# Engine orders from a list scheduler, q and k as six tokens a partition, decay as a bias of the exponentials: one change to a fused attention and channel-mix kernel

## The chip, the cores and the metric

One core of a Trainium2 chip. The metric is the device time of one execution in microseconds (us), median of several runs. A ratio leaves slow runs out: it is the mean time of one kernel's fast runs over the mean time of the kernel before's fast runs in the same rounds on the same chip, so it is not quite the ratio of the medians quoted beside it. The versions ran on several chips and in several rounds, so where two of them are close, the ratios compare them better than the medians.

## The reference, cut to what matters

```python
# q, k, v: 8 batches x 8 heads x 576 tokens x 64, float32;  f: 8 x 8 x 576
scores = scale * q @ k.T
cum    = cumsum(log(clip(f, 1e-4, 1)))
scores = where(causal, -1e9, scores + cum[i] - cum[j])     # decay
attn   = softmax(scores) @ v                               # -> x: 8 x 576 x 512
# channel mix, with x_prev = x one token earlier
xk = mu_k * x + (1 - mu_k) * x_prev;   xr likewise with mu_r
out = sigmoid(xr @ w_r) * (relu(xk @ w_k) ** 2 @ w_v)      # w_k 512x1024, w_v 1024x512, w_r 512x512
```

q and k are drawn with a standard deviation of 0.1, so the scores are tiny beside the decay.

## The kernel before

Two heads (a "pair") are worked together, 32 pairs in all, and the channel mix of a batch ("keys", "gates", "value blocks") runs between the attention of later batches. Loads arrive in float32 with one token of 64 numbers (256 bytes) as a row; other engines cast them. Decay comes in as a weight: v is multiplied by exp(-cum) on GpSimd, and the columns of E that give the row sums hold the same weights.

```python
def load(src, t, Pi, eng=None):                    # 64-number rows, float32, from SyncE's queue
    ...
        (eng or nc.sync).dma_start(out=t[:, :, hh, :],
            in_=src[b, h0 + hh, :4 * P, :].rearrange("(c p) d -> p c d", p=P))

def transposes(Pi):                                # ten 128x128 transposes, one eviction
    ...
    nc.vector.tensor_copy(qkT[Pi % NQK], tp[:, :, 0:640])          # written contiguously

def scores(Pi, ti):
    ...                                            # exponentials of both heads in one instruction
    nc.scalar.activation(out=a[:, :, off:off + w], in_=sc[:, :, 0:w], func=AF.Exp, scale=SCALE)

def vw_pair(Pi):                                   # decay into v
    nc.gpsimd.tensor_tensor(out=vw[Pi % NV], in0=vf[Pi % NV], in1=wbf[...], op=ALU.mult)

for s in range(NP + LAG):                          # the order of all engines, slot by slot
    ...
    scores(s, 0); mask(s, 0); scores(s, 1); ...
    run_gv(value_unit)
    transposes(s + 1)
    run_keys(2 * more)
    ...
```

The reciprocals of the row sums go out to DRAM once a batch and come back spread over the partitions (`scr`, then `rb`).

The softmax here doesn't subtract the row's maximum and nothing guards it: scores larger than these inputs give would overflow.

## Time and profile before

| | before |
|---|---|
| median of the first three runs | 356.54 us (354.05 to 358.79) |
| span of the profiled run | 356.4 us |
| first unit of the channel mix ("key") starts | 77.0 us |

The page, the windows, the timeline and the waits that carry the reading are quoted in the prediction. Three more groups of the page matter for what follows; the columns are line, engine, operation, output and input, shapes, count, then busy us, mean ns of one, then the idle time just before them and what ended it.

```profile
L255 ACT ACTIVATE a<-sc 128x1024 bf16<-128x1024 f32 (+2 forms) x128 | 102.2, 836 | 39.1 <-PE sc L249 39.0
L173 POOL TENSOR_TENSOR vw<-vf,wbf 128x512 bf16<-128x512 f32 x32 | 35.4, 1107 | 18.4 <-DMA vf<-in_v_dram 12.4
L192 DVE COPY qkT<-tp 128x1280 bf16<-128x1280 bf16 x32 | 26.1, 815 | 21.3 <-PE tp L191 21.3
```

The reader should note the last: one eviction of transposed q and k, 1,280 bf16 elements a partition, costs VectorE 815 ns, and there are 32.

### The profile page before, as it was taken

What the parts mean: (1) busy time and instruction counts of PE and PEld (TensorE: products, weight loads), DVE (VectorE), ACT (ScalarE), POOL (GpSimd) and SP (SyncE); (2) the same over time, 40 slices, a digit from 0 to 9 for tenths busy, and PEclk for the clock granted to TensorE, in tenths of its full rate; (3) what the DMA queues carried; (4) which work ended last, traced back from release to release, by engine and by line L of the source; (5) the groups of instructions that cost most, each with busy time, mean ns of one, the idle gap of its engine ahead of it and who ended that gap; (6) DMA issues with size and microseconds to landing.
All of it is one profiled execution on the core that took longest, in us unless ns stands there. A gap on an engine that the chain in (4) does not pass through costs nothing.

```text
span 356.4 us, 7440 instructions
## 1 busy us (share of the span) xinstructions
PE 285.3 (80%) x2853; PEld 172.9 (49%) x2853; DVE 220.2 (62%) x438; ACT 175.8 (49%) x296; POOL 158.2 (44%) x256
## 2 busy tenths in 40 slices
PE   1377573575998899888997899789978974898995
PEld 1255342354665456535664556456645542555562
DVE  5511307772889577844885889558857764558442
ACT  1567352346476556515774666356746621233451
POOL 2177375574547464725464656435653520100000
PEclk9999995669899999969999999999999989699999
DMA  9799979929963995499429971997284306420112
GB/s 162 142 180 207 200 181 209 193 56 215 197 148 89 219 234 135 104 235 187 121 81 189 235 189 62 206 228 190 62 183 114 97 17 151 93 89 31 61 59 88
DMA packets 132355, 52.02 MB, mean 146 GB/s; under 512 B 116384, under 2 KB 127136, under 8 KB 132320
## 3 DMA queue, kind: packets, MB, share of 16 engines
q1 hardware_dynamic: 128560, 48.39, 63.4%
q0 software_dynamic: 2096, 2.62, 4.5%
q10 hardware_dynamic: 1664, 0.54, 0.8%
q8 instruction: 22, 0.36, 0.5%
q14 instruction: 13, 0.11, 0.1%
HBM read 43.14 MB, written 11.01 MB: 152 GB/s over the span
## 4 chain that ended last, share of the span: by engine, by line
PE 55%; DVE 21%; DMA 11%; ACT 5%; issue 3%; SPq 3%; POOL 1%; DVEq 0%; POOLq 0%; ACTq 0%
PE kp L357 15%; PE vp L369 12%; PE rp L369 6%; PE num L322 6%; PE sc L249 5%; DMA rb<-scr 5%; PE den L282 4%; DVE xr L346 4%; PE tp L191 3%; DVE qkT L192 3%; ACT rel L361 3%; DMA kf<-in_k_dram 3%; DVE relusq L362 2%; ACT a L255 2%; PE vp L373 2%
## 5 line engine op out<-in xcount | busy, mean ns | idle before, releaser
L267 POOL TENSOR_SCALAR_AFFINE_SELECT a<-a 128x256 bf16<-128x256 bf16 (+2 forms) x128 | 68.5, 549 | 120.6 <-ACT a L255 101.0
L255 ACT ACTIVATE a<-sc 128x1024 bf16<-128x1024 f32 (+2 forms) x128 | 102.2, 836 | 39.1 <-PE sc L249 39.0
L361 ACT ACTIVATE rel<-kp 128x288 bf16<-128x288 f32 x128 | 52.6, 411 | 90.0 <-PE kp L357 84.0
L357 PE MATMUL kp<-xk,wk_sb 128*128 128x288 bf16 x512 | 79.8, 300 | 9.8 <-ACT rel L361 4.5
L249 PE MATMUL sc<-qkT 64*128 64x192 bf16 (+4 forms) x512 | 44.3, 280 | 26.0 <-DVE qkT L192 18.0
L328 DVE TENSOR_TENSOR x<-num,rb 128x384 bf16<-128x384 f32 x64 | 27.2, 458 | 59.9 <-DMA rb<-scr 38.3
L362 DVE TENSOR_TENSOR relusq<-rel 128x288 bf16<-128x288 bf16 x128 | 52.5, 430 | 18.1 <-ACT rel L361 17.7
L357 PEld LDWEIGHTS <-wk_sb 128*128 128x128 bf16 x512 | 48.9, 101 | 29.5 <-issue 14.2
L369 PE MATMUL vp<-wv_sb,relusq 128*128 128x512 bf16 x256 | 61.5, 384 | 0.0
L249 PEld LDWEIGHTS <-qkT 64*128 64x128 bf16 x512 | 23.4, 102 | 53.0 <-issue 45.3
L173 POOL TENSOR_TENSOR vw<-vf,wbf 128x512 bf16<-128x512 f32 x32 | 35.4, 1107 | 18.4 <-DMA vf<-in_v_dram 12.4
L383 ACT ACTIVATE th<-rp 128x512 f32<-128x512 f32 x36 | 21.5, 597 | 37.7 <-PE rp L369 33.8
L390 DVE SCALAR_TENSOR_TENSOR res<-th,vp 128x512 f32<-128x512 f32 x36 | 24.5, 680 | 24.1 <-PE vp L369 13.4
L192 DVE COPY qkT<-tp 128x1280 bf16<-128x1280 bf16 x32 | 26.1, 815 | 21.3 <-PE tp L191 21.3
L369 PEld LDWEIGHTS <-relusq 128*128 128x128 bf16 x256 | 23.8, 99 | 29.3 <-issue 1.6
L322 PE MATMUL num<-a,vw 128*64 128x192 bf16 (+3 forms) x448 | 31.2, 284 | 6.2 <-DVE x L328 6.2
L369 PE MATMUL rp<-wr_sb,xr 128*128 128x512 bf16 x128 | 33.7, 387 | 2.5 <-ACT rel L361 2.5
L346 DVE SCALAR_TENSOR_TENSOR xr<-diff,mu_r_sb,x 128x576 bf16<-128x576 bf16 x32 | 31.2, 976 | 0.0
L346 DVE SCALAR_TENSOR_TENSOR xk<-diff,mu_k_sb,x 128x576 bf16<-128x576 bf16 x32 | 28.4, 887 | 1.1
L191 PE MATMUL tp<-ident,qb 128*128 128x128 bf16 x128 | 14.2, 242 | 16.5 <-ACT a L255 6.7
L322 PEld LDWEIGHTS <-vw 128*64 128x64 bf16 x448 | 21.1, 119 | 13.0 <-issue 7.9
L163 POOL CAST qb<-qf 128x512 bf16<-128x512 f32 x30 | 18.7, 624 | 7.9 <-DMA qf<-in_q_dram 7.9
(55 smaller groups left out, 219.5 us busy)
## 6 DMA issues: line engine op xcount, KB each, us to landing
out_dram<-res SPq DMA_DIRECT2D x36, 256.0 KB, 2.9
qf<-in_q_dram SPq DMA_DIRECT2D x64, 128.0 KB, 4.0
vf<-in_v_dram SPq DMA_DIRECT2D x64, 128.0 KB, 3.6
kf<-in_k_dram SPq DMA_DIRECT2D x62, 128.0 KB, 4.0
rb<-scr SPq DMA_DIRECT2D x16, 384.0 KB, 5.1
rb<-scr SPq DMA_DIRECT2D x16, 192.0 KB, 5.9
scr<-R SPq DMA_DIRECT2D x8, 192.0 KB, 1.9
tail_f<-in_q_dram SPq DMA_DIRECT2D x8, 128.0 KB, 4.8
```

Source lines behind the costliest of these rows:

```text
L173: nc.gpsimd.tensor_tensor(out=vw[Pi % NV], in0=vf[Pi % NV], in1=wbf[:, :4, 2 * Pi:2 * Pi + 2].unsqueeze(3).to_broadcast([P, 4, 2, D]), op= ...
L192: nc.vector.tensor_copy(qkT[Pi % NQK], tp[:, :, 0:640])
L249: nc.tensor.matmul(sc[:, hh, col - off:col - off + n], lhsT=t[lo:lo + D, 1, kb * P:(kb + 1) * P], rhs=t[lo:lo + D, 0, q0:q0 + n], start=Tr ...
L255: nc.scalar.activation(out=a[:, :, off:off + w], in_=sc[:, :, 0:w], func=AF.Exp, scale=SCALE)
L267: nc.gpsimd.affine_select(out=v_, in_=v_, compare_op=ALU.is_ge, fill=0.0, base=0, pattern=pat, channel_multiplier=-1)
L322: nc.tensor.matmul(nm[hh * D:(hh + 1) * D, q0 - o:q0 - o + w], lhsT=t[:, kb, hh, :] if kb < 4 else tl[:, 2 * p + hh, :], rhs=a[:, hh, col: ...
L328: nc.vector.tensor_tensor(out=xs[Pi % NX][:, 1 + o:1 + o + n], in0=nm[:, 0:n], in1=rbs[Pi][:, o:o + n], op=ALU.mult)
L346: nc.vector.scalar_tensor_tensor(out=dst[:, p, :], in0=diff, scalar=mu[:, p:p + 1], in1=x[:, 0:S], op0=ALU.mult, op1=ALU.add)
L357: nc.tensor.matmul(kp[:, :HB], lhsT=wk_sb[:, db, fb * P:(fb + 1) * P], rhs=xks[b][:, db, hf * HB:(hf + 1) * HB], start=(db == 0), stop=(db ...
L361: nc.scalar.activation(rel, kp[:, :HB], func=AF.Relu)
L362: nc.vector.tensor_mul(rsq[b][:, fb, hf * HB:(hf + 1) * HB], rel, rel)
L369: nc.tensor.matmul(ps, lhsT=tiles[b][:, i, t0:t0 + P], rhs=w[:, i, :], start=(i == 0), stop=(i == n - 1))
```

## The change

Its intent: TensorE is idle for long stretches because the engines' orders are fixed slot by slot; so let a small program plan all orders from durations, dependences and buffers. Along with it come changes meant to lighten the other engines. Loads cast on the way (issued by GpSimd), q and k come six tokens to a partition, so that a row is 1,536 bytes in DRAM instead of 256, and decay becomes the bias operand of the exponential, so that v needs no scaling. The diff, cut to its core (cuts marked with three dots):

```diff
-    for s in range(NP + LAG):          # order written by hand, slot by slot
-        ...
+class Plan:                            # takes the ready step of the earliest rank ("tt") on each engine
+    def run(self, switch, bias): ...   # from durations, dependences and free buffers
+SIZES = dict(sc=2, mm=3, den=1, a=7, qkT=3, rb=2, v=5, vt=3, qk=8, rel=3, th=3, res=4, x=3, diff=2)
+SET = dict(lead=8, first=5526, fast=57, pace=6478, ... vlead=1129, qlead=4583, ...)   # ranks
+def graph(g, X=None):
+    ...
+    x = load("load_qk", (n, t), "POOL", 950, 1000 * len(pairs), ...)      # issue ns, transfer ns
+    x = load("load_v", (n,), "POOL", 1000, 1400 * len(pairs), when(i) - g["vlead"], ...)
+    EV[i].append(op("evac", (i, t), "DVE" if v else "ACT", 640 if v else 540, 130, ...))
+    ...
-        (eng or nc.sync).dma_start(out=t[:, :, hh, :], in_=...)           # float32
+        self.nc.gpsimd.dma_start(out=self.buf("qk", ("qk", n, t))[:, :w].rearrange("p h j d -> p h (j d)"),
+                                 in_=self.qk_in[t][b, h0:h0 + w].rearrange("h (p j) d -> p h (j d)", p=PT))
-            nc.tensor.transpose(tp[:, i, c * P:(c + 1) * P], in_, ident)   # 10 a pair
-    nc.vector.tensor_copy(qkT[Pi % NQK], tp[:, :, 0:640])
+                self.nc.tensor.transpose(o[hh * D:(hh + 1) * D, j * PT:(j + 1) * PT], src[:, h + hh, j, :],
+                                         self.ident, tile_position=(0, hh * D))   # 24 a pair
+    def evac(self, i, t):              # puts the tokens back in order: p*6+j <- j*96+p
+        o = self.buf("qkT", ("qkT", i))[:, t * S:(t + 1) * S].rearrange("c (p j) -> c j p", j=JT)
+        s_ = self.buf("mm", ("t", i, t)).bitcast(BF16)[:, :S].rearrange("c (j p) -> c j p", j=JT)
+        if t == 1 or i < EARLY:
+            self.nc.vector.tensor_copy(o, s_)
+        else:
+            self.nc.scalar.activation(out=o, in_=s_, func=AF.Copy)
-    nc.scalar.activation(out=a[...], in_=sc[...], func=AF.Exp, scale=SCALE)       # 4 a pair
+        self.nc.scalar.activation(out=..., in_=..., func=AF.Exp,                  # 10 a pair
+                                  bias=self.bias[:, kb, 2 * i + hh:2 * i + hh + 1], scale=1.0 / D ** 0.5)
-    nc.gpsimd.tensor_tensor(out=vw[Pi % NV], in0=vf[Pi % NV], in1=wbf[...], op=ALU.mult)
```

Batch 0 also gets its reciprocals spread by a float32 selection matmul (`pick`) instead of the trip through DRAM. The transposes leave token p·6+j at column j·96+p. The copy loops over j outside and p inside, on both sides: it reads the PSUM tile straight through and writes 2-byte elements at a step of six elements, 12 bytes.

## The prediction

> **What bounds the kernel now.** I read the page first (span, busy shares, the 40 slices, the chain), then the windows, then the timeline of one steady stretch, then the waits.
>
> ```profile
> span 356.4 us, 7440 instructions
> ...
> PE 285.3 (80%) x2853; PEld 172.9 (49%) x2853; DVE 220.2 (62%) x438; ACT 175.8 (49%) x296; POOL 158.2 (44%) x256
> ...
> PE   1377573575998899888997899789978974898995
> ...
> PEclk9999995669899999969999999999999989699999
> ...
> PE 55%; DVE 21%; DMA 11%; ACT 5%; issue 3%; SPq 3%; POOL 1%; DVEq 0%; POOLq 0%; ACTq 0%
> ```
>
> TensorE carries 55% of the chain, so no engine bounds all of it: 45% is hand-over. The slices show three stages: until about 90 us TensorE is half busy and partly at a lowered clock; then dense but not full; at the end dense with holes. The windows put numbers to it (columns: stretch, length, busy us of PE, PEld, DVE, ACT, POOL; clock; DMA share; GB/s):
>
> ```profile
> 0.00:91.00 91.00, 51.79 (x579) 34.39 (x581) 41.53 (x88) 41.79 (x54) 48.78 (x92) 0.86 0.94 175
> 91.00:290.00 199.00, 178.30 (x1902) 107.11 (x1902) 145.53 (x275) 113.23 (x197) 107.34 (x163) 0.97 0.72 156
> 290.00:356.40 66.40, 55.24 (x380) 31.39 (x380) 33.18 (x76) 20.73 (x45) 2.10 (x2) 0.94 0.25 77
> ```
>
> Busy time flatters TensorE because its records overlap. What work occupies it is better read from start to start, in the timeline and the chain in order of time (start, length, what):
>
> ```profile
> 232.37 0.61 PE L249 MATMUL sc<-qkT 64*128 64x384 bf16 x10
> ...
> 241.62 0.61 PE L249 MATMUL sc<-qkT 64*128 64x384 bf16 x10
> ...
> 245.95 0.53 PE L282 MATMUL den<-a,E 128*4 128x384 bf16 x16
> ...
> 246.41 0.85 PE L322 MATMUL num<-a,vw 128*64 128x384 bf16 x14
> ...
> 247.22 1.03 PE L357 MATMUL kp<-xk,wk_sb 128*128 128x288 bf16 x7
> ```
> ```profile
> 97.22 0.98 PE kp L357 x8
> ...
> 313.92 0.86 PE rp L369 x4
> 314.78 1.73 PE vp L369 x8
> ```
>
> Row sums take 0.46 us a pair (245.95 to 246.41), values 0.81; two key units 0.98, so 0.49 each; a gate 0.86, a value block 1.73. One pair with its share of the mix occupies a slot of 9.25 us (232.37 to 241.62). Its work: transposes 0.56, scores 0.43 and about 0.25, sums 0.46, values 0.81, four keys 1.96, 1.125 gates 0.97, 1.125 value blocks 1.95: 7.4 us. So a steady slot fills TensorE to 80%.
>
> Waits and durations used below:
>
> ```profile
> DVE x L328 <- DMA rb<-scr: 38.3, 14, 8.9
> ```
> ```profile
> 20.36 0.94 POOL L230 DMA_DIRECT2D wk_sb<-in_moe_w_k_dram  x1
> ...
> 24.65 0.77 POOL L230 DMA_DIRECT2D wr_sb<-in_moe_w_r_dram  x1
> ...
> 30.70 0.90 POOL L230 DMA_DIRECT2D wv_sb<-in_moe_w_v_dram  x1
> ```
>
> VectorE stands 38 us in 14 waits for the reciprocals that travel through DRAM, and a casting DMA costs GpSimd about 0.87 us to issue (mean of three).
>
> **What the Trainium skill says.** "Perfetto Trace Analysis", Identifying the Most-Contended Engine, says that matmul busy time is a poor measure of distance to the roofline; the trace agrees, 90% busy in the middle window against the 80% worked out above. "TensorEngine Tiling (Array Packing)", Key Properties, says that changing the tiling mode drains TensorE. The trace fits: values are 1,600 columns for each of two heads side by side, 0.67 us at the 0.86/2048 us per column of a gate, and take 0.81, so about 0.1 us goes at the change. "DMA: Bandwidth & Descriptors", SWDGE vs HWDGE vs iDMA, says that a casting DMA must be issued from GpSimd, where cores write its descriptors; hence the 0.87 us. "ScalarE: Activation LUTs", What ACT_TABLE_LOAD costs, says that a pointer operand adds about 93 ns to an ACTIVATE. The trace agrees: two of 64x576 take 682 ns without a bias tile (L203) and 774 with one (L207), 92 more. Whether this shows in back-to-back throughput no row tells.
>
> **The change part by part.**
>
> TensorE. Removed: ten 128-wide transposes a pair. Added: 24 of 96 columns on two column halves, six of them end to end per tensor: by the gate's rate 0.24 us, with many short starts I take 0.31, so 0.62 a pair against 0.56. Scores use the same 1,600 columns a head (0.7 us), but the first four pairs do the heads apart (four times 0.43 more). Sums and values have the same columns. The boundary block at row 512 of two batches becomes an ordinary one. Batch 0 gets eight fp32 selections, about 4 us together, in place of a trip through DRAM. Sum without drains: keys 128 x 0.49 = 62.7; gates 36 x 0.86 = 31; value blocks 36 x 1.73 = 62.3; attention 32 x (0.62 + 0.70 + 0.40 + 0.70) = 77.4; early heads 1.7; selections and bias 4.5: 240 us. Mode changes: I count about six a pair (transposes, values, scores twice, sums, back to full size), 32 x 6 x 0.1 = 19 us. TensorE needs about 259 us. So the arithmetic is not what shrinks; the idle time is.
>
> Start. Before, the mix starts at 91 us. Now decay needs no scaled v and no weighted sum columns, exponentials start as soon as the bias is there, the scheduler sends eight pairs ahead, and batch 0 normalises after two pairs and without DRAM. My estimate for the first key unit: bias at about 10 us, four pairs of exponentials at 3.4 to 4.3 us each until about 26, norm, selection and four pairs of mixing on VectorE (about 2.9 us a pair by its rows) until 33 to 38. In this time TensorE has about 18 us of attention work, so some 16 us are lost, where the first 91 us of before lost some 60.
>
> Middle and end. Reciprocals are asked for long before they are needed, so the 38 us of waits should go. The two engine orders are merged by a scheduler that knows a duration for each step; static buffers (seven exponential tiles, eight q/k tiles, rings of 3) let attention run ahead. At the end only the last block's chain remains: evict, store with 2.9 us to landing: 4 us. The 12 us hole at 294 to 305, one trip through DRAM, is covered by queued mix.
>
> GpSimd. Removed: casts 18.9 + 18.7 + 8.3, scaled v 35.4 + 8.3, in all 90 us. Added: 34 q/k loads, 64 v loads, 8 tails, 5 weights at 0.87 us: 97 us. Masks become 160: 128 at 0.50 and 32 at 0.42, 77 us for 68.5. About 178 us: no relief, though below 259. Loads of q and k go from 73,728 rows of 256 B to 12,288 of 1,536 B.
>
> ScalarE. The forms 128x1024, 128x768, 128x384 last 1023, 806, 493 ns: 0.83 ns a column and 175; two back to back take 1.94 us, so an instruction occupies 0.83 a column and about 72. Ten a pair of 3,200 columns in all: 3.37 us, 108 in total. The bias tile may add 92 ns each, 29 us. With 128 relus at 0.31, 36 tanh at 0.5, 28 evictions at 0.55 and the spreads: 183 to 212 us.
>
> VectorE. Squares go from 128 (52.5 us) to 64 of 128x576 at about 0.52 (33 us); scaling wv and the casts go, four more evictions come: about 200 us.
>
> Sum: 259 of TensorE + 16 at the start + 4 at the end = 279 with perfect packing. Against that, six mode changes a pair may be too many (some fall into idle time, some steps lie side by side): minus 8. For imperfect packing in the middle I add 2%, 5 us. Predicted: 276 us.
>
> **The rivals.**
>
> A, the ScalarE bound: if the bias operand costs throughput, a pair with its share of relu, tanh and eviction takes about 6.6 us while attention runs; TensorE needs about 7.9. So it would be a near second and disturb the order: 280 to 290 us. For it: 92 ns more in L207. Against: there was no neighbour to overlap with.
>
> B, GpSimd's queue: masks stand in order behind load issues. If an issue costs well over 0.87 us (a v load has 512 short pieces), or is held at a buffer, masks come late, sums and values wait, and the static order stalls: 290 to 310 us. For it: the scheduler's table gives one v group of four loads 1.0 us where these rows say 3.5. Against: 1,024 pieces of weights cost no more than 512.
>
> C, short transposes do not overlap: 24 weight loads a pair at about 56 ns rather than 26 add 0.7 us a pair, 23 us: near 298 us.
>
> D, packing is better than I grant: if drains mostly vanish and the first keys start by 28 us, 255 to 262 us.
>
> **Range and chances.** D and a mild A or C span 258 to 296 us. To reach the old time minus 2%, 349 us, idle time would have to stay at 90 us of 349, which needs two rivals at full size. Faster 0.95, same 0.03, slower 0.02.
>
> **What would show it.** Keys starting near 35 us; TensorE's share of the chain above 75%; the wait of VectorE for the reciprocals near zero; a steady pair with its mix in about 8 us; clock near full after 30 us. A is right if exponentials follow each other at over 0.6 us for 576 columns; B if GpSimd's issue rows exceed 100 us and TensorE waits for masks; C if transposes of one tensor take over 0.5 us. I am wrong altogether if start-to-start times of keys and value blocks grow, or if the start still takes over 60 us.

## The result, and the profile after

| | before | after |
|---|---|---|
| median (4 runs each, same chip) | 355.83 us (354.05 to 358.79) | 372.75 us (371.63 to 373.39) |
| ratio, 95% interval | | 1.045 (1.0386 to 1.0514): slower |

The prediction, 276 us, was wrong by 97 us and in its sign. Head of the page of the changed kernel, its slices of TensorE, and its chain by engine:

```profile
span 369.9 us, 8111 instructions
...
PE 293.9 (79%) x3141; PEld 167.9 (45%) x3141; DVE 235.9 (64%) x376; ACT 260.3 (70%) x525; POOL 151.2 (41%) x281
...
PE   2463597589859888689589986888878899999995
...
PEclk9999998879987999999989996999989999999998
...
PE 51%; ACT 25%; DVE 13%; issue 5%; POOL 4%; DMA 1%; ACTq 0%; DVEq 0%; POOLq 0%
```

TensorE's share of the chain fell from 55% to 51%, and ScalarE, 5% before, now holds 25% of it. The slices show a start of some 75 us at about half density, as before, then mostly eights and nines. ScalarE's busy time went up by 84.5 us (175.8 to 260.3). Two of the groups below raised it, the exponentials (102.2 us before) and ScalarE's share of the evictions; the one between them holds VectorE's evictions:

```profile
L490 ACT ACTIVATE a<-sc,bias 128x576 bf16<-128x576 f32 (+2 forms) x320 | 155.1, 545 | 52.1 <-PE sc L468 50.3
...
L461 DVE COPY qkT<-mm 128x576 bf16<-128x576 bf16 x36 | 73.5, 2082 | 30.0 <-PE mm L454 24.9
...
L463 ACT ACTIVATE qkT<-mm 128x576 bf16<-128x576 bf16 x28 | 58.5, 2089 | 5.5 <-PE mm L454 4.8
```

An eviction of 576 elements takes 2.08 us on either engine, where 1,280 elements took 0.815 us before. All 64 cost 132 us of two engines instead of 26 us of one. What that does to the order is in the chain in order of time (start, length, what), of the changed kernel in its middle:

```profile
81.06 2.09 ACT qkT L463
...
88.60 1.26 ACT a L490 x2
89.87 1.98 ACT qkT L463
91.84 1.00 ACT a L490 x2
...
97.03 1.26 ACT a L490 x2
98.30 1.97 ACT qkT L463
```

Once a pair the path runs through ScalarE: two exponentials, the eviction, two exponentials. Nothing behind the eviction in ScalarE's order starts for 2 us. And until it ends, the eviction holds the PSUM buffer that it reads, one of three (`mm`) that transposes, keys, gates and value blocks share. The timeline of a later stretch shows a key unit waiting for just such a buffer (in brackets: idle before, and what ended it):

```profile
192.80 2.09 ACT L463 ACTIVATE qkT<-mm 128x576 bf16<-128x576 bf16 x1
...
194.95 1.63 PE L591 MATMUL mm<-xk,wk 128*128 128x288 bf16 x12 [1.38 <-ACT qkT L463]
```

To see the whole span in one sum I split it by the start times of the trace's matmuls. A matmul that lasts over 1.15 times the usual of its form counts as run at half clock, and half of its time is the loss; a gap is from the modelled end of one matmul to the start of the next. The usual is the form's median. This is an estimate, good to a few us. In us:

| | before | after | loops exchanged (e1) | order searched (e14) |
|---|---|---|---|---|
| before the first matmul | 5.6 | 5.4 | 5.4 | 5.2 |
| TensorE's work at full clock | 256.1 | 267.3 | 267.8 | 270.1 |
| lost to half clock | 28.8 | 26.1 | 24.8 | 19.1 |
| gaps up to 80 us | 30.0 | 29.1 | 27.7 | 15.3 |
| gaps after 80 us | 31.7 | 37.4 | 14.7 | 7.1 |
| after the last matmul | 3.8 | 4.1 | 4.1 | 4.1 |
| span of the profiled run | 356.4 | 369.9 | 344.9 | 321.0 |

The first column of differences, before to after, says where the 13.5 us came from: 11 us more work on TensorE and 6 us more gaps after 80 us, against 3 us less loss to the clock. And it says where the expected gain did not appear: the gaps at the start stayed at 29 us, and those of the middle, which the scheduler was to close, grew.

### The profile page after: what moved, and what is told of

Read it like the earlier page. It is cut to its first block, busy times and chain, and to the rows that moved or that the text cites.

```text
span 369.9 us, 8111 instructions
## 1 busy us (share of the span) xinstructions
PE 293.9 (79%) x3141; PEld 167.9 (45%) x3141; DVE 235.9 (64%) x376; ACT 260.3 (70%) x525; POOL 151.2 (41%) x281
## 4 chain that ended last, share of the span: by engine, by line
PE 51%; ACT 25%; DVE 13%; issue 5%; POOL 4%; DMA 1%; ACTq 0%; DVEq 0%; POOLq 0%
PE mm L616 15%; PE mm L591 14%; ACT a L490 11%; ACT qkT L463 11%; PE sc L468 7%; PE mm L606 6%; DVE qkT L461 6%; PE mm L556 4%; PE mm L454 3%; POOL a L497 2%; ACT rel L595 2%; PE den L512 2%; DVE x L564 1%; PE mm L527 1%; POOL v L404 1%
## 5 line engine op out<-in xcount | busy, mean ns | idle before, releaser
L490 ACT ACTIVATE a<-sc,bias 128x576 bf16<-128x576 f32 (+2 forms) x320 | 155.1, 545 | 52.1 <-PE sc L468 50.3
L497 POOL TENSOR_SCALAR_AFFINE_SELECT a<-a 128x256 bf16<-128x256 bf16 (+1 forms) x160 | 70.1, 454 | 128.4 <-ACT a L490 122.9
L461 DVE COPY qkT<-mm 128x576 bf16<-128x576 bf16 x36 | 73.5, 2082 | 30.0 <-PE mm L454 24.9
L591 PE MATMUL mm<-xk,wk 128*128 128x288 bf16 x512 | 76.3, 293 | 11.8 <-ACT qkT L463 11.3
L616 PE MATMUL mm<-wv,sq 128*128 128x512 bf16 x288 | 74.6, 403 | 2.9 <-ACT qkT L463 2.6
L595 ACT ACTIVATE rel<-mm 128x288 bf16<-128x288 f32 x128 | 52.4, 429 | 27.3 <-PE mm L591 23.8
L468 PE MATMUL sc<-qkT 64*128 64x64 bf16 (+4 forms) x384 | 47.9, 301 | 25.3 <-ACT a L490 13.7
L591 PEld LDWEIGHTS <-wk 128*128 128x128 bf16 x512 | 49.2, 100 | 35.0 <-issue 16.7
L463 ACT ACTIVATE qkT<-mm 128x576 bf16<-128x576 bf16 x28 | 58.5, 2089 | 5.5 <-PE mm L454 4.8
L404 POOL DMA_DIRECT2D v<-in_v_dram x64 | 47.8, 765 | 9.5 <-PE mm L556 3.9
L626 DVE SCALAR_TENSOR_TENSOR res<-th,mm 128x512 f32<-128x512 f32 x36 | 25.3, 703 | 29.1 <-PE mm L616 24.3
L564 DVE TENSOR_TENSOR x<-mm,rb 128x384 bf16<-128x384 f32 (+1 forms) x64 | 27.7, 466 | 16.1 <-PE mm L556 12.8
L512 PE MATMUL den<-a,ones 128*4 128x192 bf16 (+4 forms) x512 | 19.4, 263 | 11.3 <-POOL a L497 11.3
```

Of the source, the lines that this page charges most:

```text
L404: self.nc.gpsimd.dma_start(out=t[:, :, h, :], in_=self.v_in[b, h0 + h, :4 * P, :].rearrange("(c p) d -> p c d", p=P))
L461: self.nc.vector.tensor_copy(o, s_)
L463: self.nc.scalar.activation(out=o, in_=s_, func=AF.Copy)
L468: self.nc.tensor.matmul(o, lhsT=t[lo:lo + D, S + kb * P:S + (kb + 1) * P], rhs=t[lo:lo + D, q0:q0 + n], start=True, stop=True)
L490: self.nc.scalar.activation(out=self.buf("a", ("a", i))[:, hh, KOFF[kb]:KOFF[kb] + n], in_=self.buf("sc", ("s", i, tok))[:, o:o + n], func ...
L497: self.nc.gpsimd.affine_select(out=v_, in_=v_, compare_op=ALU.is_ge, fill=0.0, base=0, pattern=[[0, 2], [1, n]], channel_multiplier=-1)
```

## The experiments

Theories are named by a letter in the expectations. W: the stepped write into SBUF makes the evictions slow (its rival R: it is a stepped access in general, so a stepped read costs the same). E: the slow evictions explain the loss (its rival P: the packing, that is the planned order itself, is bad). A: the bias operand of the exponentials costs ScalarE its throughput. Q: the loads issued by GpSimd hold up the masks that stand behind them in its order. All versions start from the changed kernel unless said otherwise.

### The evictions

**e1_swap**: the same copy with its two loops exchanged. It now writes contiguously and reads PSUM at a step of 96 elements. The same elements go to the same places.

```diff
-        o = self.buf("qkT", ("qkT", i))[...].rearrange("c (p j) -> c j p", j=JT)
-        s_ = self.buf("mm", ("t", i, t))...rearrange("c (j p) -> c j p", j=JT)
+        o = self.buf("qkT", ("qkT", i))[...].rearrange("c (p j) -> c p j", j=JT)
+        s_ = self.buf("mm", ("t", i, t))...rearrange("c (j p) -> c p j", j=JT)
```

> The changed kernel with the loop order of the 64 q/k evictions exchanged: results still right, now the write into SBUF is contiguous and the read from PSUM takes the step of 96 elements. Theory W (the 2-byte writes at a step of 12 bytes cost the 3.6 ns an element): an eviction falls from 2.08 us to about 0.7 us and the kernel to 270 to 310 us. Theory R (any 2-byte access of this pattern that is not contiguous on one side costs the same): evictions stay at 2 us and the time at 373 us, within 2%.

Measured: 346.35 us, ratio 0.976 (0.9704 to 0.9817), correct. The two groups of evictions:

```profile
L461 DVE COPY qkT<-mm 128x576 bf16<-128x576 bf16 x36 | 26.6, 744 | 35.7 <-PE mm L454 28.9 <-PE sc L468 6.2 <-ACT a L490 0.5
...
L463 ACT ACTIVATE qkT<-mm 128x576 bf16<-128x576 bf16 x28 | 18.3, 653 | 7.1 <-PE mm L454 6.5 <-PE sc L468 0.6
```

2,082 ns became 744, and 2,089 became 653. So R is out. The step is not slow as such: it is slow on the side that writes SBUF, and far less so, at 96 elements, on the side that reads PSUM. Two changed lines turn a loss of 4.5% into a gain of 2.4%. The evictions did what W said, but the kernel did not come to the 270 to 310 us expected with it: 26 of the 97 us by which the prediction missed go with the evictions, and some 70 stay.

**e2_plain**: no reordering at all, contiguous on both sides. The tokens of q and k are then scrambled.

```diff
-        o = ....rearrange("c (p j) -> c j p", j=JT);  s_ = ....rearrange("c (j p) -> c j p", j=JT)
+        o = self.buf("qkT", ("qkT", i))[:, t * S:(t + 1) * S]
+        s_ = self.buf("mm", ("t", i, t)).bitcast(BF16)[:, :S]
```

> The changed kernel with the 64 q/k evictions as plain contiguous copies: tokens stay in the transposed order, so the result is wrong on purpose, while every instruction, size and wait is otherwise the same. Theory E (the slow evictions are the whole of the miss): an eviction takes 0.6 to 0.7 us, VectorE and ScalarE lose about 50 us and 40 us of busy time, and the kernel takes 265 to 290 us, near my prediction. Theory P (the static order was laid out for other durations, above all for exponentials without the price of the bias operand, and stays loose whatever the evictions cost): 300 to 340 us.

Measured: 343.74 us, ratio 0.9686 (0.9636 to 0.9737).

```profile
L461 DVE COPY qkT<-mm 128x576 bf16<-128x576 bf16 x36 | 15.8, 445 | 37.8 <-PE mm L454 30.2 <-PE sc L468 7.1 <-ACT a L490 0.5
```

VectorE's copy takes 445 ns, ScalarE's 653 as in e1. So this stepped read of PSUM costs VectorE 300 ns and ScalarE nothing, and that remnant is worth about 3 us of the kernel (the two intervals overlap). Theory E, 265 to 290 us, is refuted: even free of the reordering the kernel stays some 68 us above the prediction, and just above the 300 to 340 us of theory P. The comparison called the result correct although the tokens are scrambled; it can't see this at such small scores. The correctness of e1 rests on the two access patterns naming the same pairs of elements, not on that comparison.

**e11_before_step**: the opposite test, in the kernel before. Its one eviction a pair is made to write at a step of five elements (10 bytes); the result is scrambled, nothing else changes.

```diff
-        nc.vector.tensor_copy(qkT[Pi % NQK], tp[:, :, 0:640])
+        nc.vector.tensor_copy(qkT[Pi % NQK].rearrange("q t (p j) -> q t j p", j=5),
+                              tp[:, :, 0:640].rearrange("q t (j p) -> q t j p", j=5))
```

> One part of the change alone, in the kernel before: its q/k eviction (32 copies of 2 x 640 columns, 0.82 us each) writes at a step of 5 elements of 2 bytes; the tokens are mixed up (wrong on purpose, though the check may not see it, since the scores are tiny beside the decay). If the step of the write is what costs 3.6 ns an element, the copy takes about 4.6 us, VectorE gains some 120 us of busy time and becomes the bound: 400 to 460 us. If the cost belongs to something else in the changed kernel, the copy stays near 0.8 to 1.4 us and the time within 5% of 356.

Measured: 428.29 us, the median of two fast and two slow runs; the fast ones took 421.51 and 426.42 us, ratio 1.1879 (1.1758 to 1.2). The group, of the fast run that was profiled, whose time before was 815 ns:

```profile
L192 DVE COPY qkT<-tp 128x1280 bf16<-128x1280 bf16 x32 | 118.6, 3707 | 14.8 <-PE tp L191 14.8
```

Fast runs with fast, the write step alone makes the kernel before some 67 us slower. Per element it is 3707/1280 = 2.9 ns here and 2082/576 = 3.6 ns in the changed kernel. The Trainium skill, "SBUF — State Buffer", Specifications (TRN2), says of SBUF's 16-byte cachelines: "need ≥2 hits per line for full bandwidth; each cross to a new line pays a penalty". The runs agree in direction. They fit a price per line entered as well: a step of 12 bytes enters a new line for 12/16 of the elements, one of 10 bytes for 10/16, so 3.6/0.75 = 4.8 ns and 2.9/0.625 = 4.6 ns a line. That is an estimate from two points and the page's line size. No run varied the step further or tried elements of another size, so a price per line is not shown.

### The rows of q and k

**e3_rows**: what the slow write bought was long DRAM rows. Here q and k come in rows of 256 bytes instead, token j·96+p to partition p, in one load per head, and the eviction is plain and right.

```diff
-        self.nc.gpsimd.dma_start(out=...("p h j d -> p h (j d)"), in_=...("h (p j) d -> p h (j d)", p=PT))
+        for h in range(w):
+            self.nc.gpsimd.dma_start(out=o[:, h], in_=self.qk_in[t][b, h0 + h].rearrange("(j p) d -> p j d", p=PT))
```

> The changed kernel with q and k loaded as 256-byte rows (128 casting loads of one head instead of 34 of up to four heads) so that the transposes give tokens in order and the eviction is contiguous: right result. If theory E holds and GpSimd's queue can bear 94 more issues at about 0.7 us (66 us more on 151), it stays within 5% of the plain-copy run; if GpSimd becomes the bound or its masks come late, it is 10% or more above that run, with TensorE waiting for masks or for q and k.

Measured: 370.93 us, ratio 1.0464 (1.0405 to 1.0524), correct: 27 us slower than e2, which differs only in the loads. The issues of q's loads on GpSimd, in place of 17 at 688 ns:

```profile
L398 POOL DMA_DIRECT2D qk<-in_q_dram x64 | 46.6, 740 | 5.4 <-PE mm L455 3.5 <-POOLq L673 0.9 <-issue 0.4
```

With k's 64 issues GpSimd is busy 218.1 us instead of 151.9, the first mask comes at 51.1 us instead of 38.0, and the first key at 94.9 us instead of 72.1. So few loads of long rows are worth keeping, as long as the order is restored on the read side. The bytes are the same, so it is more than bytes that holds the start; whether it is the number of issues or the shorter rows this run does not separate.

### The bias operand

**e4_plain_nobias**: e2 with the exponentials' bias operand left out. The result is wrong (relative error 0.76).

```diff
-                                  bias=self.bias[:, kb, 2 * i + hh:2 * i + hh + 1], scale=1.0 / D ** 0.5)
+                                  scale=1.0 / D ** 0.5)
```

> The plain-copy kernel with the exponentials' bias operand left out as well (wrong result on purpose, second cause). Rival A (the bias operand costs throughput on ScalarE): an exponential of 576 columns is followed by the next 0.09 us sooner, ScalarE loses about 30 us of busy time, and the kernel is 10 us or more faster than the plain-copy run. If A is false or ScalarE is off the path, the two are within 2%.

Measured: 338.9 us, ratio 0.9566 (0.9493 to 0.964), so 5 us less than e2; the intervals just touch.

```profile
L490 ACT ACTIVATE a<-sc 128x576 bf16<-128x576 f32 (+2 forms) x320 | 123.1, 447 | 68.5 <-PE sc L468 63.8
```

546 ns (e2) became 447, 99 less each, and ScalarE's busy time fell from 225.2 to 200.5 us. In the traces, where one exponential of 576 columns follows another without a gap, the median from start to start is 639 ns with the operand and 547 without (49 cases each). So what it adds stays in full when instructions follow each other. But ScalarE is not the bound once its evictions are short: 25 us less work on it go with 5 us. Even these are not shown to come from it. By the split used above, TensorE's work and gaps are as in e2 within 1 us, and the 5 us are less time lost to half clock (16.9 us for 22.4).

### GpSimd's loads and the masks behind them

In the changed kernel GpSimd issues loads until 38 us. The timeline of that engine alone:

```profile
29.03 0.74 POOL L404 DMA_DIRECT2D v<-in_v_dram  x1 [0.72 <-DMA qk<-in_k_dram]
...
30.45 5.96 POOL L404 DMA_DIRECT2D v<-in_v_dram  x8
...
38.55 2.19 POOL L497 TENSOR_SCALAR_AFFINE_SELECT a<-a 128x256 bf16<-128x256 bf16 x6
```

The exponentials that the first masks need end at 18.1 us, but the first mask runs at 38.5. The issues before it are not only many: the first line shows one that waited 0.72 us for an earlier load of k to land. The trace's semaphores say why. GpSimd's 111 loads take eight completion semaphores in turn, so from the ninth on a load waits until the eighth before it has landed, and everything behind it in GpSimd's order waits too.

**e6_vlate**: e1 with v's loads ranked some 9 us later, which lets masks go first.

```diff
-... vlead=1129, ...
+... vlead=-8000, ...
```

> On top of the exchanged loop order: one number of the scheduler's table changed, so that the v loads are ranked about 9 us later on GpSimd (vlead 1129 to -8000). Theory Q (at the start GpSimd's in-order queue is held by loads, each of which from the ninth on waits until the eighth before it has landed, and the masks stand behind them until 38 us): the first mask comes at 15 to 25 us, the first key unit before 65 us instead of 72, and the kernel is 6 to 15 us faster than the 346 us of the exchanged order alone. If the start is bound by something else (bytes of q, k, v, ScalarE, or the clock of TensorE), it stays within 2% of it.

Measured: 345.1 us, ratio 0.9668 (0.9614 to 0.9721); e1 had 0.976. So the 6 to 15 us expected did not come; the two intervals overlap. The first mask came forward to 18.8 us, as expected, yet the first key went back from 72.3 to 88.3 us. The chain before it runs through a load of w_v that took 12.4 us to land, the v loads that waited for it until 41 us, and twelve more v loads between 72 and 83 us. Gaps of TensorE: 39.4 us for e1's 42.4. One rank moves the queue's trouble from one place to another.

**e10_pick**: e1 with the clearing of the selection tile moved to the front of the set-up. GpSimd needs that tile after its first two loads and the identity, before any other load, and in the changed kernel it waits 5.0 us for VectorE to clear it.

```diff
 def setup_early(self):
+        nc.vector.memset(self.pick, 0.0)
 def setup_late(self):
-        nc.vector.memset(self.pick, 0.0)
```

> On top of the exchanged loop order: the clearing of the selection matrix moves from the late to the early set-up, so that GpSimd does not stand from 3.4 to 8.3 us before the second pair's loads. If those 5 us are on the path that sets the end (theory Q, the chain of waits of the plain-copy run shows them as issue time), the kernel is 3 to 5 us faster than 346; if the start has slack there, no change (within 1%).

Measured: 342.09 us, ratio 0.9581 (0.9527 to 0.9635). First mask at 34.7 us (e1: 38.2), first key at 69.2 (72.3): 3 to 4 us earlier, and the whole kernel gains rather more than that by its ratio, 1.8%, with intervals that don't overlap. It is the base of the next versions.

**e12_quarterv** and **e13_halfissues**: how much the v loads cost. Both clear v's buffers once and give wrong results. The first issues all 64 loads with a quarter of the pieces each (128 of 512); the second issues every second load in full.

```diff
 # e12
-            self.nc.gpsimd.dma_start(out=t[:, :, h, :], in_=self.v_in[b, h0 + h, :4 * P, :]...)
+            self.nc.gpsimd.dma_start(out=t[:, :1, h, :], in_=self.v_in[b, h0 + h, :P, :]...)
 # e13
-        for h in range(2 * len(pairs)):
+        for h in range(0, 2 * len(pairs), 2):
```

> On top of the exchanged loop order and the early clearing (342 us): the same 64 v loads, but each fetches only the first of its four chunks (128 pieces instead of 512; the rest of the buffers is zeroed once; wrong result on purpose). GpSimd issues as often, the DMA engines move a quarter of the pieces. If what holds the start is the transfers (each load waits for the eighth before it to land), it gains more than halving the number of loads does: 8 us or more. If it is GpSimd's issue time alone, it gains under 3 us.

> The counterpart: only every second head's v is loaded, so 32 loads instead of 64 at full size (half the issue time, half the pieces; wrong result on purpose). If GpSimd's issue time holds the masks at the start, it gains 8 us or more and more than the run with a quarter of the pieces. If the start is bound elsewhere, both stay within 2% of 342 us.

Measured: 325.44 us, ratio 0.9113 (0.9075 to 0.915), and 320.57 us, ratio 0.8963 (0.8915 to 0.9012). Beside e10 that is 17 and 22 us. The first mask comes at 30.8 and 27.2 us, the first key at 62.4 and 62.7. The v loads of e12 and then e13 on GpSimd (e10: 64 issues of 767 ns):

```profile
L406 POOL DMA_DIRECT2D v<-in_v_dram x64 | 34.4, 558 | 6.6 <-PE mm L558 3.6
```
```profile
L406 POOL DMA_DIRECT2D v<-in_v_dram x32 | 24.0, 757 | 5.8 <-PE mm L558 3.5
```

A quarter of the pieces also made each issue shorter, 558 ns for 767, and half the loads move half the pieces, so the two runs do not separate issue time from pieces. Together they show that the loads of v are worth about 20 us in the planned order (by the split, some 6 of them less half clock), though GpSimd is busy less than half of the span. It is the engine that is least busy and yet holds the others.

### The plan: durations, limits and ranks

**e8_plan** and **e15_plan_pick**: the planner's durations set to what the trace shows (exponentials 95 ns longer, q and k issues 680 ns, a v group 1,490 ns of issue and 2,900 ns of transfer for each pair), with the ranks as they were. The first starts from e1, the second from e10.

```diff
-            for kb, occ in ((0, 545), (1, 438)):
+            for kb, occ in ((0, 640), (1, 533)):
-        x = load("load_v", (n,), "POOL", 1000, 1400 * len(pairs), ...)
+        x = load("load_v", (n,), "POOL", 1490 * len(pairs), 2900 * len(pairs), ...)
   ...                                     # the other exponentials and load_qk likewise
```

> On top of the exchanged loop order: the scheduler's table gets durations as the trace shows them (exponentials 95 ns longer for the bias operand, a q/k issue 0.68 us, a v group 1.49 us of GpSimd and 2.9 us of transfer a pair); nothing else is changed, only the order on each engine follows. Theory P (a static order laid out for wrong durations is what keeps it loose): at least 2% faster than the 346 us of the exchanged order alone. If the order was good enough, or the ranks and not the durations decide it, it stays within 2%.

> The two small gains together: early clearing and the table with the trace's durations, ranks as they were. If they are separate (5 us of GpSimd at the start; a better order in the middle), 337 to 340 us; if they are the same microseconds, 342.

Measured: 343.06 us, ratio 0.9623 (0.956 to 0.9685), and 343.03 us, ratio 0.9609 (0.9561 to 0.9657). The first is 1.4% better than e1 (0.976), short of the 2% that theory P in the form of durations asked for; the second is no better than e10 (0.9581), so the gains of durations and of early pick do not add up. Right durations alone leave the kernel at 343 us.

**e14_search14**: e10 with those durations, with two limits added to the planner, and with new ranks. The limits: at most eight loads of GpSimd in flight, and TensorE at half speed for the first 45 us. The ranks come from a random search for the plan with the earliest end by the planner's own reckoning; only this one plan was tried on the chip.

```diff
+SIZES = dict(lane=8, ...)                        # every GpSimd load holds a "lane" until it lands
+            t[o.eng] = o.start + o.occ * (2 if o.eng == "PE" and o.start < 45000 else 1)
-SET = dict(lead=8, first=5526, fast=57, pace=6478, dlag=4368, tlead=15956, ..., vlead=1129, qlead=4583, ...)
+SET = dict(lead=6, first=21432, fast=1681, pace=3740, dlag=7427, tlead=-1047, ..., vlead=-14383, qlead=9634, ...)
```

> A candidate for the best version: exchanged loop order, early clearing, and the scheduler's ranks found anew by a random search against its table with the durations of the trace, the eight-in-flight limit of the loads on GpSimd and half-rate matmuls for the first 45 us. If the order is what is left to gain (theory P), it beats 342 us by 3% or more; if the work of TensorE and the start set the time, it stays within 2%.

Measured: 322.52 us (321.23 to 322.94), ratio 0.9018 (0.898 to 0.9056), correct. This version beats both kernels. Its page:

```profile
span 321.0 us, 8079 instructions
...
PE 62%; ACT 12%; DMA 9%; DVE 8%; issue 3%; POOL 2%; SPq 1%; DVEq 0%; POOLq 0%; ACTq 0%
```

TensorE has 62% of the chain. The first mask runs at 14.2 us. The first key starts at 69.5 us, no earlier than in e10 (69.2). What differs is what TensorE does until then; the first window of each, e10 and then e14 (stretch, length, busy us of PE, PEld, DVE, ACT, POOL; clock; DMA share; GB/s):

```profile
0.00:80.00 80.00, 49.69 (x580) 28.54 (x581) 33.51 (x76) 48.19 (x107) 60.02 (x105) 0.94 1.10 126
```
```profile
0.00:80.00 80.00, 59.51 (x686) 34.59 (x687) 36.81 (x84) 57.07 (x126) 54.41 (x102) 0.94 0.92 128
```

Ten us more of TensorE's work lie in the first 80 us, attention that later need not be done. The time of the first key, by which I had meant to judge the start, is the wrong sign to look for.

**e16_model_oldranks**: e14's planner, with the same durations and limits, but the old ranks. It tells the ranks from the model.

```diff
   (e14)
-SET = dict(lead=6, first=21432, ...)
+SET = dict(lead=8, first=5526, ...)              # as in the change
```

> The version whose pick memset is early, with all three corrections of the planner that the searched version has (durations as the trace shows them, at most eight loads of GpSimd in flight, TensorE at half rate for the first 45 us) but with the old ranks. Theory P in the form 'the ranks': the better model alone brings little, so 335 to 346 us, ratio to the kernel before 0.94 to 0.97, near the 342 and 343 us of the two versions with the old ranks. Rival, 'the model': a planner that sees the limits packs better whatever its ranks, 318 to 328 us, ratio 0.89 to 0.92, as the searched version had (322.5). My weight: 0.7 to the first.

Measured: 339.17 us, ratio 0.9497 (0.9426 to 0.9568), correct. The expectation held: of the 20 us between e10 and e14 the model alone brings 3, and the new ranks on top of it 17. But it is no flat 3. In gaps of TensorE, worked out as above, the start is as good as e14's (15.6 us up to 80 us, first mask at 17.5), and 10 us better than e10's 25.3; the rest gives 7 of them back (20.1 us against e10's 12.9 and e14's 7.1). A good part of that is one place near the end, which the chain in time shows:

```profile
292.45 1.87 DMA scr<-R
...
294.98 5.61 DMA rb<-scr
```

There TensorE has run out of mix to do while the last batch's reciprocals go through DRAM, as in the kernel before at 294 to 305 us.

**e17_search_step**: e14 with the stepped write put back in its evictions.

```diff
-        o = ....rearrange("c (p j) -> c p j", j=JT);  s_ = ....rearrange("c (j p) -> c p j", j=JT)
+        o = ....rearrange("c (p j) -> c j p", j=JT);  s_ = ....rearrange("c (j p) -> c j p", j=JT)
```

> The searched version with the evictions put back to the stepped write that the change has (2.1 us each instead of 0.65 to 0.75), everything else as searched. If the 64 slow evictions cost their full weight in any order (theory E, about 28 us between the changed kernel and the version with the loops exchanged), 322.5 + 25 to 32, so 348 to 355 us, ratio 0.97 to 0.995. If a better order hides part of them (they need 90 us more of VectorE and ScalarE, which stand idle 40% and 29% of the span in the searched version), 330 to 345 us, ratio 0.925 to 0.965. Over 0.995 would say that the searched order is brittle: it was planned with short evictions.

Measured: 362.94 us, ratio 1.02 (1.0134 to 1.0266), correct. This lay outside what I had thought likely. The slow evictions cost 40 us here, more than the 26 us between the changed kernel and e1, and the wait view names them:

```profile
PE mm L589 <- ACT qkT L461: 14.1, 12, 1.6
```

TensorE's key units stand 14.1 us in 12 waits for evictions of q and k. They share no data, but they share PSUM: the plan, run from the kernel's source, gives the key unit of each of the 12 the very `mm` buffer that the eviction has to empty (all 9 such waits in the changed kernel, 11.3 us, too). A tight order has less slack for slow evictions; that the loose one hid some is my reading. No run gave `mm` a fourth buffer or the transposes one of their own. Hence also a caution: what a part is worth depends on the order it is tried in, and the 26 and the 17 us above are worths in their place, not constants that add up.

## Why the prediction was wrong, point by point

The split of the span by terms shows where 276 us and the profiled 369.9 us part. It is 94 us: 16 in TensorE's work, 26 in a term that was missing, 51 in idle time, and none at the end.

**TensorE's work: 259 us, less 8.** The count of 259 was good: 267.3 measured. The "minus 8" for mode changes that fall into idle time was not; I count some 250 changes in the executed order, not 192. At the prediction's own 0.1 us each, an estimate, they make 240 without changes into 265. The rival C, slow short transposes, was false: a pair's 24 transposes take about 0.65 us against 0.62. (Its sign, over 0.5 us for one tensor, does show in the start, 0.62 to 0.69 us, but there TensorE ran at half clock.)

**The clock.** The sum had no term for half clock, though it was the prediction that quoted a lowered clock in the start. 26 us are lost there after, 29 before. In the changed kernel three score matmuls of one head take 1.03 us early on; later six take 0.61, two heads side by side, with the same 1,024 columns for each head:

```profile
14.19 1.03 PE L468 MATMUL sc<-qkT 64*128 64x512 bf16 x3 [6.40 <-DVE qkT L461]
```
```profile
190.95 0.61 PE L468 MATMUL sc<-qkT 64*128 64x512 bf16 x6
```

The Trainium skill, "TensorE: Matmul & The Clock Gate", Part 1: The HAM clock gate, says that the array runs at half rate by default and at full rate only after sustained activity. The start agrees: its matmuls come in short bursts, and two thirds of the loss (17 of 26 us) fall before 80 us. The page's row of the granted clock shows nines for the first 55 us, where 13 us of it fall, for the trace's first record of the clock is at 53.9 us; before that only durations show it. All of the rest lies in six stretches of 3 to 7 us that the trace records at half clock. "Clock near full after 30 us" was wrong.

**The start: 16 us.** The gaps up to 80 us are 29, and 5.4 us pass before the first matmul. The first key, predicted for 33 to 38 us, came at 74.3, so the start took the over 60 us that the prediction had named as a sign of being wrong altogether. (In the kernel before the first key runs at 77.0 us, not at the prediction's 91.) Three things were missed. Every eviction is 2.08 us instead of the 0.55 to 0.8 that my rows gave; exchanging the loops brings the first key only to 72.3. The plan that the change carries, run from its source, has the first key at 51 us itself, which the prediction doesn't mention. And the masks wait behind GpSimd's loads. That is rival B, and its mechanism was right: e12 and e13 show 17 and 22 us, and its own guess of a rise to 290 to 310 us fits a cost of that size. The other half of its sign came, too: TensorE's row sums stand 11.3 us for masks. But the first half was badly chosen. The issue rows add up to some 81 us, not "over 100", for an issue costs 0.67 to 0.77 us and not 0.87; the harm lies in where they stand and in the eight loads in flight, not in their sum. Even with half the loads of v gone (e13) the first key comes at 62.7 us, so what holds it beyond the plan's 51 us is only in part accounted for.

**The middle: 5 us.** Gaps after 80 us are 37 us, of which 23 go when the evictions' loops are exchanged, and 30 in e14. This is the step that failed worst, and it failed in the account of ScalarE and VectorE: "28 evictions at 0.55" and "four more evictions come". Those numbers were read from copies that write contiguously; the rearrangement in the diff was taken for free. 28 × 2.09 and 36 × 2.08 add some 90 us to the two engines. ScalarE came to 260 us instead of the 183 to 212 predicted, and TensorE waits for the PSUM buffers that the evictions hold and for what stands behind them. None of my four rivals contained this. The other part of the 37 us is the plan: with the loops exchanged 15 us of gaps stay, which e14, with early pick, the corrected model and new ranks, brings to 7. The Trainium skill states the penalty in words and I didn't look for it, for I had asked what each operation costs and not what each access pattern costs.

**What was right.** The reciprocals' wait on VectorE (38.3 us before) is gone from the page, and the hole near 294 us is covered: 2.7 us of gaps between 280 and 320 us, where the kernel before had 8.2. The bias tile costs what was said, 92 ns more from one exponential of 576 columns to the next. So rival A was right about throughput, and its sign came (639 ns, over 0.6 us), but with the evictions mended it is worth 5 us at most. The end costs 4 us as predicted.

**The planner's word.** I took it that a scheduler with a duration for each step would pack within 2%. By its own reckoning (the plan run from the kernels' sources) the change's plan ends at 302 us, and it says 0.64 and 0.54 us for an eviction, so it shared my error. With e1's loops and early pick it is still 38 us short of the profiled span (302 against 340); with the corrected durations and limits and old ranks 12 (325 against 337.6); and after the search 3 (318 against 321). So here plan and chip came together as the slow steps were mended and the model was checked against the trace.

Open is how the cost of a stepped write goes with the step beyond two points, how far the ranks of e14 are from the best, and whether a search with the unchecked model would have found ranks as good: no run tried it.

## What to carry to other kernels

Before a change trades one access pattern for another, ask for each instruction at what step it writes SBUF: a 2-byte write at 12 bytes was three times as slow as the same copy with its loops exchanged, and it turned a gain into a loss. In a static order an engine that is mostly idle can still hold the rest, so keep loads that wait for other loads off the queue that carries work on the path. Check a planner's durations and limits against a trace before searching over its ranks; the new ranks gave 17 of the last 20 us here, found with a model that had the limits.

## What the Trainium skill lacked or had wrong

- "SBUF — State Buffer", Specifications (TRN2), names the penalty for entering a new 16-byte line but gives no price. These runs: 2,082 ns (VectorE) and 2,089 ns (ScalarE) for 576 bf16 elements written at a step of 12 bytes, 445 and 653 ns contiguous; 3,707 for 815 ns with 1,280 elements at 10 bytes.
- No page says what a stepped read of PSUM costs ScalarE: nothing here, 653 ns with a step of 96 elements and 653 without (e1 and e2).
- "ScalarE: Activation LUTs", What ACT_TABLE_LOAD costs, gives about 93 ns for a pointer operand and an overlap of about 93 ns for ACTIVATEs back to back, without saying whether the operand's time is what overlaps. Here it is not: 639 ns from start to start with it, 547 without.
- "DMA: Bandwidth & Descriptors", SWDGE vs HWDGE vs iDMA, doesn't mention that in a kernel built as this one GpSimd's loads share eight completion semaphores, so that a load whose eighth predecessor is in flight stalls the compute instructions behind it: first mask at 38.5 us in the changed kernel, at 14.2 us where the order allowed for it. An issue took 0.67 to 0.77 us.
- "TensorE: Matmul & The Clock Gate", Part 1, holds, but for this kernel its remark that the ramp is below 1% of a typical span does not: TensorE ran at half clock for most of the first 50 us, and 12 to 15 us of 321 to 370 were lost there (before, changed, e1, e14). With later stretches at half clock the loss is 19 to 29 us.
